# Block-sparse attention with a gated feed-forward layer on one core: value products in column halves, joint maxima, transposes without layout copies

## The chip, the cores and the metric

The kernel runs on one core of a Trainium2 chip. The core has a matrix engine (TensorE, called PE in the profile, with its weight loads as PEld), a vector engine (DVE), a scalar engine (ACT), a general engine (POOL) and a queue engine (SP). They run side by side, each taking its own instructions in the order in which the program lists them, and wait for each other by semaphores. TensorE writes to PSUM, eight banks of 512 fp32 columns on 128 partitions; DVE and ACT read it. The metric is the device time of one execution in microseconds.

## The reference

For 4 batches and 8 heads, 768 tokens and a head width of 64, scores are computed block by block (32 tokens). A row of blocks sees its own block, its neighbours, the first and the last block, and three sampled blocks. The first and the last row see everything. After the softmax and the product with V, the tokens go through a feed-forward layer with the activation h * sigmoid(beta * h).

```
scores = q @ k^T / sqrt(64)
mask = |bi - bj| <= 1  or  bi, bj in {0, 23}  or  bj in sampled[bi]
attn = softmax(where(mask, scores, -1e9));   x = attn @ v
x = x as [3072 tokens, 512]
h = x @ w_in            # [3072, 2048]
out = (h / (1 + exp(-beta * h))) @ w_out
```

## The kernel before

All work is described as tasks (class `Task`, lines 23 to 33) with an engine, an assumed duration, a priority, the tasks they depend on, and the PSUM banks that they open and close. `Plan.run` (lines 51 to 179) plays the tasks through once on the host and so fixes the order of every engine's instructions and the bank of every result: at each moment a free engine takes the task of the lowest priority number whose inputs and banks are there; a task whose banks are not free is passed over. The feed-forward tasks may hold at most 4 of the 8 banks while attention is left.

**Preparation of a batch.** K, Q and V arrive as fp16, 128 partitions by [head, 6 x 64], each partition holding six tokens. Batches 1 to 3 are loaded by POOL's queue in two halves each (line 443) into two buffers `RAW`, where Q takes V's. DVE copies (line 447) turn K and Q into `K16` and `Q16`, [6, 512] on each partition, so that two heads lie side by side. For batch 0 the loads go over SP and the cast from fp32 does the same (line 397). For each pair of heads, six full transposes on TensorE (lines 463 to 466) then fill a bank, and ACT or DVE copies it into `KT` or `QT` (line 470). V is rearranged by DVE (`vperm`), written to a table in device memory (`vtab`, line 494) and gathered from there for each pair of block rows over SP's queue (line 582).

**A pair of block rows**, n = 0 to 43, eleven in each batch:
- POOL and DVE gather eight K blocks for each row (`kg`, `kn`, lines 515 to 547).
- `sc` (line 595): 8 matmuls write the mask (L600) and 16 the scores (L610). Each uses 64 rows and 32 columns of the array at a tile position of its own; the heads of even and odd number (u = 0, 1) go to a bank each.
- `mx` (line 621): for each of the two banks one reduce on DVE, 128 partitions by 512, gives two negated maxima.
- `ex` (line 627): for each bank two exponentials on ACT with a sum each (L629).
- `rc`, `nrm`: reciprocal on DVE, four multiplications, mostly on POOL (L641).
- `tp`, `ptv`: eight transposes (L653), one copy out of PSUM (L657).
- `av` (line 661): 16 value products (L668). The stationary operand holds two heads' V, 128 columns; the moving one both heads' weights, 64 columns. Of the [128, 64] result only the blocks where the heads agree are used: rows 0 to 63 with columns of u = 0, rows 64 to 127 with those of u = 1.
- `xv` (line 678): the two useful quarters are therefore copied to `xT` one by one, 64 partitions by 256, each by DVE or ACT (L259 and L257, the lines of the helper `copy_on`).

**Global rows** (the first and the last block row, four units a batch, lines 691 to 777): scores over all 768 keys in two banks a unit (L705), two reduces of 384 and a third that joins them (L719, L721), two exponentials (L726), a sum and a reciprocal (L733, L734), a multiplication (L737), transposes (L745), and for the batch 24 products with V (`gav`, L758), copied to `xT` in four parts.

**Feed-forward**, in eight groups of 8 or 16 block rows: 16 slices of h (`h`, L817, 4 matmuls each), tanh on ACT (L823), the gate on DVE (L828), and per 128 tokens 64 matmuls into the output (`y`, L845), ACT's scaling (L263) and an output DMA on ACT's queue (L863). The activation is computed as h/2 * (1 + tanh(beta h / 2)).

Of the kernel before, what the change touches and what calls it, by code (L numbers as in the profile page):

```python
# [22 lines left out]
class Task:  # L23
    def __init__(self, name, eng, dur, emit, deps=(), prio=0.0, lat=0.0,
                 opens=(), closes=(), moe=False, dma=0.0, slack=0.0, hw=0, bulk=None):
        self.on = {eng: dur} if isinstance(eng, str) else dict(eng)
        self.name, self.eng, self.dur, self.emit = name, None, None, emit
        self.deps = [d for d in deps if d is not None]
        self.prio, self.lat = prio, lat
        self.opens, self.closes, self.moe, self.dma = opens, closes, moe, dma  # L30
        self.slack, self.hw, self.bulk = slack, hw, bulk
        self.kind = name.rstrip("0123456789.")
        self.end = None


class Plan:
# [9 lines left out]
    def add(self, *a, **k):  # L46
        t = Task(*a, **k)
        self.tasks.append(t)
        return t

    def run(self):
# [36 lines left out]
        while done < len(tasks):  # L88
            progress = False
            for e in engines:  # L90
# [3 lines left out]
                for t in waiting[e]:  # L94
# [9 lines left out]
                    if t.opens:  # L104
                        n_ok = sum(1 for f, _ in bank_free if f <= now + 1e-9)
                        if n_ok < len(t.opens):
                            continue
                        if t.moe and attention_left and held_moe + len(t.opens) > self.moe_banks:
                            continue
# [8 lines left out]
                if t.opens:  # L118
                    bank_free.sort()
                    for name in t.opens:  # L120
                        _, i = bank_free.pop(0)
# [61 lines left out]
def kernel(  # L183
# [14 lines left out]
    BLK = 32  # L198
# [32 lines left out]
    K16 = sb("K16", [P, J, D_MODEL])  # L231
    Q16 = sb("Q16", [P, J, D_MODEL])
    RAW = [sb(f"RAW{i}", [P, H, J * D]) for i in range(2)]
# [14 lines left out]
    banks = [psum.tile([P, 512], FP32, name=f"bank{i}") for i in range(8)]  # L248
# [4 lines left out]
    bank16 = lambda name: banks[plan.bank[name]][:, :].bitcast(FP16)  # L253

# [131 lines left out]
    for i, (nm, t, dst) in enumerate((("K", k, K16), ("Q", q, Q16), ("V", v, None))):  # L386
        for f in range(2):
# [6 lines left out]
            for hp in range(2 * f, 2 * f + 2):  # L394
# [3 lines left out]
                        out=dst[:, :, hp * P:(hp + 1) * P].rearrange("p j (h d) -> p h j d", h=2),  # L398
                        in_=stage32(i, hp).rearrange("p h (j d) -> p h j d", j=J)),
# [31 lines left out]
    trK, trQ, evK, evQ, vperm, vtab, perm = {}, {}, {}, {}, {}, {}, {}  # L431
    later = {b: [] for b in range(B)}
    for b in range(B):
        pr = prep_prio(b)
        if b:
            vperm[b] = []
            for nm, t, raw, dst in (("V", v, RAW[0], Vn[b % 2]), ("K", k, RAW[1], K16), ("Q", q, RAW[0], Q16)):
                tr = {"K": trK, "Q": trQ}.get(nm)
                for f in range(2):
                    hs = slice(f * HH, (f + 1) * HH)  # L440
                    free = [vperm[b][f]] if nm == "Q" else [perm["QK"["VK".index(nm)], b - 1, f]] if b > 1 else []
# [5 lines left out]
                    tpm = add(f"perm{nm}{b}.{f}", "DVE", 0.55, lambda raw=raw, dst=dst, hs=hs: copy_on(  # L447
                        "DVE", dst[:, :, hs.start * D:hs.stop * D].rearrange("p j (h d) -> p h j d", h=HH),
                        raw[:, hs, :].rearrange("p h (j d) -> p h j d", j=J)),
                        deps=[tl] + ([tr[b - 1, hp] for hp in range(2 * f, 2 * f + 2)] if tr else []),  # L450
                        prio=pr - 5 * (nm == "V"))
                    if nm == "V":
                        vperm[b].append(tpm)
                    else:
                        perm[nm, b, f] = tpm
                        for hp in range(2 * f, 2 * f + 2):
                            ld[nm, b, hp] = tpm
        for nm, s16, dstT, tr, ev in (("K", K16, KT, trK, evK), ("Q", Q16, QT, trQ, evQ)):
            for hp in range(NHP):
                def emit_tr(nm=nm, s16=s16, b=b, hp=hp):  # L460
                    o = bank16((nm, b, hp))
                    for j in range(J):
                        nc.tensor.transpose(  # L463
                            out=o[:, j * P:(j + 1) * P],
                            in_=s16[:, j, hp * P:(hp + 1) * P],
                            identity=identity)
# [36 lines left out]
    for n, (b, p) in enumerate(order_pairs):  # L503
# [91 lines left out]
        def emit_sc(n=n, b=b, p=p, i0=i0, kgb=kgb):  # L595
# [11 lines left out]
            for g in range(2):  # L607
                for hp in range(NHP):
# [9 lines left out]
                    opens=(("S", n, 0), ("S", n, 1)))  # L618

        for u in range(2):  # L620
            mx[n, u] = add(f"mx{n}.{u}", "DVE", 0.6, lambda n=n, u=u, sb_=sb_: nc.vector.tensor_reduce(  # L621
                out=sb_[:, 0, 2 * u:2 * u + 2],
                in_=bank(("S", n, u))[:, :].rearrange("x (g c) -> x g c", g=2),
                axis=AX.X, op=ALU.max, negate=True),
                deps=[sc[n]] + ([nrm[n - NP]] if n >= NP else []), prio=pr)

# [6 lines left out]
            ex[n, u] = add(f"ex{n}.{u}", "ACT", 0.91, emit_ex, deps=[mx[n, u]] + (  # L633
# [27 lines left out]
        def emit_av(n=n, vgb=vgb):  # L661
            o = bank(("O", n))
            pt = PT[n % NPT].rearrange("x (g c u m) -> x g c u m", g=2, c=2, u=2)
            first = True
            for g in range(2):
                for hp in range(NHP):
                    for c in range(2):
                        nc.tensor.matmul(  # L668
                            o[:, (g * NHP + hp) * 64:(g * NHP + hp + 1) * 64],
                            lhsT=vgb[:, g, c, hp * P:(hp + 1) * P],  # L670
                            rhs=pt[:, g, c, :, hp * BLK:(hp + 1) * BLK],
                            start=first, stop=(c == 1), skip_group_check=True)
                        first = False
        av[n] = add(f"av{n}", "PE", 0.47, emit_av, deps=[ptv[n], vres] + vg[n], prio=pr - 0.5, lat=0.2,
                    opens=(("O", n),))
        evs = []
        for u in range(2):
            def emit_xv(eng, n=n, u=u, b=b, i0=i0):
                src = bank(("O", n))[u * D:(u + 1) * D, :].rearrange(
                    "x (g h v m) -> x g h v m", g=2, h=NHP, v=2)[:, :, :, u, :]  # L680
                c0 = x_of(b * NB + i0)
                dst = xT[u * D:(u + 1) * D, :, c0:c0 + 2 * BLK].rearrange(
                    "x h (g m) -> x g h m", g=2)
                copy_on(eng, dst, src)
            evs.append(add(f"xv{n}.{u}", {"DVE": 0.42, "ACT": 0.38}, None, emit_xv, deps=[av[n]], prio=pr - 0.5,
                           closes=(("O", n),)))
# [7 lines left out]
    for b in range(B):  # L694
        for w, (blk, u) in enumerate((bl, u) for bl in (0, NB - 1) for u in range(2)):
# [15 lines left out]
            if u == 0:  # L711
                gs = add(f"gs{m}", "PE", 0.5, emit_gs, deps=[evK[b, hp] for hp in range(NHP)] +
                         [evQ[b, hp] for hp in range(NHP)], prio=pr, lat=0.2,
                         opens=tuple(("GS", m + uu, hf) for uu in range(2) for hf in range(2)))
                gsc_all.setdefault(b, []).append(gs)

            def emit_gm(m=m, s_=s_):
                for hf in range(2):
                    nc.vector.tensor_reduce(out=s_[:, hf:hf + 1], in_=bank(("GS", m, hf))[:, 0:S // 2],  # L719
                                            axis=AX.X, op=ALU.max, negate=True)  # L720
                nc.vector.tensor_reduce(out=s_[:, 2:3], in_=s_[:, 0:2], axis=AX.X, op=ALU.min)  # L721
            gm = add(f"gm{m}", "DVE", 1.15, emit_gm, deps=[gs] + ([gn[m - 2]] if m >= 2 else []), prio=pr)

            def emit_ge(m=m, s_=s_, pg=pg):
                for hf in range(2):
                    nc.scalar.activation(  # L726
                        out=pg[:, hf * (S // 2):(hf + 1) * (S // 2)], in_=bank(("GS", m, hf))[:, 0:S // 2],
                        func=AF.Exp, bias=s_[:, 2:3], scale=1.0, accum_out=s_[:, 3 + hf:4 + hf])
            ge = add(f"ge{m}", "ACT", 1.12, emit_ge, deps=[gm] + ([gt[m - 2]] if m >= 2 else []), prio=pr,
                     closes=(("GS", m, 0), ("GS", m, 1)))  # L730

            def emit_gr(s_=s_):
                nc.vector.tensor_reduce(out=s_[:, 5:6], in_=s_[:, 3:5], axis=AX.X, op=ALU.add)  # L733
                nc.vector.reciprocal(out=s_[:, 6:7], in_=s_[:, 5:6])  # L734
            gr = add(f"gr{m}", "DVE", 0.26, emit_gr, deps=[ge], prio=pr)
            gn[m] = add(f"gn{m}", {"POOL": 0.9, "DVE": 0.44}, None, lambda eng, s_=s_, pg=pg: (
                nc.vector if eng == "DVE" else nc.gpsimd).tensor_scalar(  # L737
                out=pg, in0=pg, scalar1=s_[:, 6:7], scalar2=1.0, op0=ALU.mult, op1=ALU.mult),
# [14 lines left out]
        def emit_gav(b=b):  # L753
            o = bank(("GO", b))
            first = True
            for hp in range(NHP):
                for j in range(J):
                    nc.tensor.matmul(  # L758
                        o[:, hp * P:(hp + 1) * P], lhsT=Vn[b % 2][:, j, hp * P:(hp + 1) * P],
                        rhs=PTG[:, j, :, hp * BLK:(hp + 1) * BLK],  # L760
                        start=first, stop=(j == J - 1), skip_group_check=True)
                    first = False
        gavt[b] = add(f"gav{b}", "PE", 1.4, emit_gav, deps=[gptv[gun - 4 + w] for w in range(4)] +
                      vperm[b], prio=pr, lat=0.2, opens=(("GO", b),))
        evs = []
        for u in range(2):
            def emit_gx(eng, u=u, b=b):
                src = bank(("GO", b))[u * D:(u + 1) * D, :].rearrange(
                    "x (h k v m) -> x h k v m", h=NHP, k=2, v=2)
                for kk, blk in enumerate((0, NB - 1)):  # L770
                    c0 = x_of(b * NB + blk)
                    dst = xT[u * D:(u + 1) * D, :, c0:c0 + BLK]
                    copy_on(eng, dst, src[:, :, kk, u, :])
            evs.append(add(f"gx{b}.{u}", {"DVE": 0.55, "ACT": 0.5}, None, emit_gx, deps=[gavt[b]], prio=pr,
                           closes=(("GO", b),)))
# [128 lines left out]
```

## Time and profile before

| | us |
|---|---|
| median of 3 runs | 320.73 (320.28 to 332.21) |
| the profiled execution | 323.59 |
| span of its instructions | 321.8 |
| PE busy | 280.7 |
| DVE busy | 246.7 |
| ACT busy | 216.8 |
| POOL busy | 187.5 |
| granted TensorE clock, mean | 0.929 |

The span reaches from the first to the last instruction of the profiled execution. Busy time is the time in which an engine had at least one instruction in flight; for TensorE, where matmuls are pipelined, it is more than the time in which the next could not have started. L and a number is a line of the kernel's file. A group's entry reads: line, engine, operation, output <- inputs, shapes, count, busy us and mean ns of one, idle time of the engine before these instructions, and what ended that. The chain of waits is followed back from the last instruction: at each step to what released it, or to the instruction before it on its engine.

### The profile page before, as it was taken

To read this page: it belongs to the slowest core of one execution; us is meant where nothing else is said; L and a number is where in the kernel's file an instruction comes from. 1 tells how busy PE (TensorE), PEld (TensorE's weight loads), DVE (VectorE), ACT (ScalarE), POOL (GpSimd) and SP (SyncE) were. 2 spreads that over 40 slices of the span, in tenths; PEclk is the share of its full clock that TensorE was granted. 3 is DMA by queue.
4 is the path that set the end of the run, shared out by engine and by line. 5 is a ranking of instruction groups with operands and counts; after the bars stand their busy time and mean duration, and the time that the engine had idled before them with its cause. 6 is when DMAs were issued, how large, how long until landed. Compare 5 with 4: busy or idle time off the path is not lost.

```text
span 321.8 us, 10665 instructions
## 1 busy us (share of the span) xinstructions
PE 280.7 (87%) x3525; PEld 177.3 (55%) x3525; DVE 246.7 (77%) x572; ACT 216.8 (67%) x644; POOL 187.5 (58%) x528
## 2 busy tenths in 40 slices
PE   0845578989979699988979999999999999999994
PEld 0612366956755486556635656555665555554671
DVE  2996579878869989999987667999979975771060
ACT  1676435864968489789687669977679864772361
POOL 2479956848778456798966654756948453200000
PEclk9975557999979989999979999999999999999999
DMA  7889995998697586323777973335232333100201
GB/s 255 332 172 208 229 227 105 187 252 177 132 204 145 164 212 114 107 80 94 125 146 168 226 170 93 88 84 153 94 118 69 91 110 100 33 3 33 98 2 66
DMA packets 42211, 43.97 MB, mean 137 GB/s; under 512 B 6440, under 2 KB 37672, under 8 KB 42156
## 3 DMA queue, kind: packets, MB, share of 16 engines
q1 hardware_dynamic: 27760, 25.71, 27.1%
q0 software_dynamic: 10784, 11.27, 23.4%
q10 hardware_dynamic: 3612, 6.30, 5.4%
q8 instruction: 28, 0.46, 0.6%
q14 instruction: 27, 0.22, 0.2%
HBM read 45.10 MB, written 9.44 MB: 169 GB/s over the span
## 4 chain that ended last, share of the span: by engine, by line
PE 60%; DMA 14%; DVE 12%; ACT 6%; issue 3%; SPq 3%; POOL 1%; POOLq 0%; ACTq 0%; DVEq 0%
PE bank L845 22%; PE bank L817 21%; DMA VG<-VT 6%; PE bank L668 4%; PE bank L653 4%; DMA RAW<-in_k_dram 3%; DMA VT<-Vn 3%; SPq L582 3%; DVE ST L621 2%; ACT PP L629 2%; PE bank L463 2%; DVE g L828 2%; PE bank L610 2%; PE bank L600 2%; DMA sbl<-in_sampled_blocks_dram 1%
## 5 line engine op out<-in xcount | busy, mean ns | idle before, releaser
L641 POOL TENSOR_SCALAR PP<-PP,ST 128x256 f16<-128x256 f16 x168 | 81.3, 501 | 47.9 <-DVE ST L635 42.4
L629 ACT ACTIVATE PP<-bank,ST 128x256 f16<-128x256 f32 x176 | 81.6, 478 | 30.1 <-DVE ST L621 21.5
L817 PE MATMUL bank<-xT,w_in_sb 128*128 128x256 f16 (+1 forms) x512 | 97.1, 338 | 3.9 <-ACT PP L629 1.1
L845 PE MATMUL bank<-w_out_sb,g 128*128 128x512 f16 x384 | 90.9, 380 | 0.0
L828 DVE SCALAR_TENSOR_TENSOR g<-t,bank 128x512 f16<-128x512 f16 (+1 forms) x128 | 66.6, 546 | 22.1 <-ACT t L823 21.3
L823 ACT ACTIVATE t<-bank,beta_sb 128x512 f16<-128x512 f32 (+1 forms) x128 | 69.9, 589 | 14.3 <-PE bank L817 11.6
L817 PEld LDWEIGHTS <-w_in_sb 128*128 128x128 f16 x512 | 55.3, 116 | 30.1 <-issue 8.6
L521 POOL COPY KG<-KT 128x64 f32 x264 | 54.6, 256 | 24.6 <-PE bank L610 17.8
L621 DVE TENSOR_REDUCE ST<-bank 128x2 f32<-128x512 f32 x88 | 57.5, 678 | 7.5 <-PE bank L610 7.4
L845 PEld LDWEIGHTS <-g 128*128 128x128 f16 x384 | 34.7, 98 | 38.6 <-issue 4.1
L668 PE MATMUL bank<-PT,VG 128*128 128x64 f16 x704 | 31.8, 199 | 7.9 <-DMA VG<-VT 5.9
L668 PEld LDWEIGHTS <-VG 128*128 128x128 f16 x704 | 28.3, 102 | 16.5 <-issue 9.6
L629 ACT ACTIVATION_READ_ACCUMULATOR PP<-bank,ST 128x1 f32 x176 | 36.8, 209 | 0.0
L653 PE MATMUL bank<-identity,PP 128*128 128x128 f16 x352 | 30.9, 233 | 6.6 <-ACT xT L257 2.4
L653 PEld LDWEIGHTS <-PP 128*128 128x128 f16 x352 | 24.6, 104 | 15.9 <-issue 4.1
L657 DVE COPY PT<-bank 128x1024 f16<-128x1024 f16 x44 | 30.1, 684 | 4.1 <-PE bank L653 3.3
L259 DVE CAST xT<-bank 64x256 f16<-64x256 f32 (+1 forms) x52 | 20.6, 402 | 12.3 <-PE bank L668 7.5
L263 ACT ACTIVATE osb<-bank 128x512 f32<-128x512 f32 x24 | 14.4, 601 | 20.7 <-PE bank L845 20.7
L257 ACT CAST xT<-bank 64x256 f16<-64x256 f32 (+1 forms) x52 | 17.4, 346 | 15.4 <-DVE xT L259 6.3
L610 PE MATMUL bank<-KG,QT 64*32 64x256 f16 x704 | 20.9, 293 | 1.4 <-POOL KG L521 1.0
L726 ACT ACTIVATE PG<-bank,SG 128x384 f16<-128x384 f32 x32 | 18.4, 583 | 4.9 <-DVE SG L721 4.1
L600 PE MATMUL bank<-maskr,ones 64*32 64x192 f16 (+1 forms) x352 | 14.9, 272 | 5.7 <-ACT PP L629 5.5
(79 smaller groups left out, 256.6 us busy)
## 6 DMA issues: line engine op xcount, KB each, us to landing
VG<-VT SPq DMA_DIRECT2D x268, 32.0 KB, 2.6
VG<-VT SPq DMA_DIRECT2D x40, 192.0 KB, 2.9
out_dram<-osb ACTq DMA_DIRECT2D x20, 256.0 KB, 2.2
RAW<-in_v_dram POOLq DMA_DIRECT2D x6, 384.0 KB, 5.1
RAW<-in_k_dram POOLq DMA_DIRECT2D x6, 384.0 KB, 5.6
VT<-Vn SPq DMA_DIRECT2D x3, 768.0 KB, 6.1
RAW<-in_q_dram POOLq DMA_DIRECT2D x6, 384.0 KB, 6.5
w_in_sb<-in_moe_w_in_dram POOLq DMA_DIRECT2D x8, 256.0 KB, 5.9
```

The lines of the kernel that those rows point to most:

```text
L521: nc.gpsimd.tensor_copy(out=kg32[:, g, :, (2 + r) * W:(3 + r) * W], in_=kt32[:, :, bass.ds(vals[3 * g + r], W)])
L610: nc.tensor.matmul(bk[u][hp * BLK:(hp + 1) * BLK, g * 256:(g + 1) * 256], lhsT=QT[b % 2][u * D:(u + 1) * D, hp, (i0 + g) * BLK:(i0 + g + 1 ...
L621: mx[n, u] = add(f"mx{n}.{u}", "DVE", 0.6, lambda n=n, u=u, sb_=sb_: nc.vector.tensor_reduce(out=sb_[:, 0, 2 * u:2 * u + 2], in_=bank(("S" ...
L629: nc.scalar.activation(out=pb[:, u, g, :], in_=bank(("S", n, u))[:, g * 256:(g + 1) * 256], func=AF.Exp, bias=sb_[:, 0, 2 * u + g:2 * u + ...
L641: (nc.vector if eng == "DVE" else nc.gpsimd).tensor_scalar(out=pb[:, u, g, :], in0=pb[:, u, g, :], scalar1=sb_[:, 2, 2 * u + g:2 * u + g + ...
L653: nc.tensor.transpose(out=o[:, s * P:(s + 1) * P], in_=pb[:, u, g, c * P:(c + 1) * P], identity=identity)
L657: ptv[n] = add(f"ptv{n}", "DVE", 0.61, lambda n=n: nc.vector.tensor_copy(out=PT[n % NPT], in_=bank16(("T", n))), deps=[tp[n]] + ([av[n - N ...
L668: nc.tensor.matmul(o[:, (g * NHP + hp) * 64:(g * NHP + hp + 1) * 64], lhsT=vgb[:, g, c, hp * P:(hp + 1) * P], rhs=pt[:, g, c, :, hp * BLK: ...
L817: nc.tensor.matmul(o[:, 0:TW], lhsT=w_in_v[:, c, f // 4, f % 4, :], rhs=xT[:, c, c0:c0 + TW], start=(c == 0), stop=(c == NHP - 1))
L823: lambda G=G, f=f, TW=TW, tt=tt: nc.scalar.activation(out=tt[:, 0:TW], in_=bank(("H", G, f))[:, 0:TW], func=AF.Tanh, bias=0.0, scale=beta_ ...
L828: lambda G=G, f=f, TW=TW, tt=tt, gg=gg: nc.vector.scalar_tensor_tensor(out=gg[:, f, 0:TW], in0=tt[:, 0:TW], scalar=1.0, in1=bank(("H", G, ...
L845: nc.tensor.matmul(o[:, :], lhsT=gg[:, f, s * P:(s + 1) * P], rhs=w_out_sb[:, f, :], start=(f == 0), stop=(f == N_FFC - 1))
```

## The change

Three things are done differently.

**Value products in two column halves.** `av` and `gav` issue two matmuls for each one of before, each for one head alone: 64 stationary columns, and 32 (64 for `gav`) moving ones, at tile positions (0, 0) and (0, 64). The useful results now fill 256 columns on all 128 partitions, and one copy takes them to `xT`. The last block row is computed ahead of the first, so that the global rows' two blocks are adjacent in `xT`.

**Joint maxima over two adjacent banks.** The banks become four tiles of two. `sc` and `gs` ask for pairs of adjacent banks (`twin=True`), which `choose` hands out; single banks are taken from broken pairs first. One reduce of 128 by 1024 gives a pair's four maxima, and both banks' exponentials wait for it. A global unit has one reduce, one exponential over 768 columns and one reciprocal.

**K and Q are transposed head by head as loaded.** The layout copies of K and Q are gone, and so are `K16` and `Q16`. Each head's [128, 64] piece is transposed by itself, 12 matmuls for a pair of heads, to 64 partitions each. K, Q and V have a buffer each; a half of K's or Q's is free for the next batch when its transposes are done.

The durations that the planner assumes stay at 0.36 us for a pair of heads' transposes, 0.47 for `av` and 1.4 for `gav`.

```diff
+    @staticmethod
+    def choose(t, bank_free, now):
+        at = {i: f for f, i in bank_free if f <= now + 1e-9}
+        whole = sorted((max(at[i], at[i + 1]), i) for i in at if i % 2 == 0 and i + 1 in at)
+        if t.twin:
+            if 2 * len(whole) < len(t.opens):
+                return None
+            return [i + h for _, i in whole[:len(t.opens) // 2] for h in range(2)]
+        if len(at) < len(t.opens):
+            return None
+        return sorted(at, key=lambda i: ((i ^ 1) in at, at[i], i))[:len(t.opens)]
...
-    K16 = sb("K16", [P, J, D_MODEL])
-    Q16 = sb("Q16", [P, J, D_MODEL])
-    RAW = [sb(f"RAW{i}", [P, H, J * D]) for i in range(2)]
+    RK, RQ, RV = (sb(f"R{x}", [P, H, J * D]) for x in "KQV")
...
-                    free = [vperm[b][f]] if nm == "Q" else [perm["QK"["VK".index(nm)], b - 1, f]] if b > 1 else []
+                    if tr is None:
+                        free = [vperm[b - 1][f]] if b > 1 else []
+                    else:
+                        free = [tr[b - 1, hp] for hp in hps]
...
                     for j in range(J):
-                        nc.tensor.transpose(
-                            out=o[:, j * P:(j + 1) * P],
-                            in_=s16[:, j, hp * P:(hp + 1) * P],
-                            identity=identity)
+                        for u in range(2):
+                            nc.tensor.transpose(
+                                out=o[u * D:(u + 1) * D, j * P:(j + 1) * P],
+                                in_=s16[:, 2 * hp + u, j * D:(j + 1) * D],
+                                identity=identity, tile_position=(0, u * D))
...
+        mx[n] = add(f"mx{n}", "DVE", 1.2, lambda n=n, sb_=sb_: nc.vector.tensor_reduce(
+            out=sb_[:, 0, :], in_=twin(("S", n, 0))[:, :, :].rearrange("x u (g c) -> x (u g) c", g=2),
+            axis=AX.X, op=ALU.max, negate=True),
+            deps=[sc[n]] + ([nrm[n - NP]] if n >= NP else []), prio=pr)
...
                     for c in range(2):
-                        nc.tensor.matmul(
-                            o[:, (g * NHP + hp) * 64:(g * NHP + hp + 1) * 64],
-                            lhsT=vgb[:, g, c, hp * P:(hp + 1) * P],
-                            rhs=pt[:, g, c, :, hp * BLK:(hp + 1) * BLK],
-                            start=first, stop=(c == 1), skip_group_check=True)
-                        first = False
+                        for u in range(2):
+                            us = slice(u * D, (u + 1) * D)
+                            nc.tensor.matmul(
+                                o[us, (g * NHP + hp) * BLK:(g * NHP + hp + 1) * BLK],
+                                lhsT=vgb[:, g, c, (2 * hp + u) * D:(2 * hp + u + 1) * D],
+                                rhs=pt[:, g, c, u, hp * BLK:(hp + 1) * BLK],
+                                start=(g + hp + c == 0), stop=(c == 1), skip_group_check=True,
+                                tile_position=(0, u * D))
...
-        for u in range(2):
-            def emit_xv(eng, n=n, u=u, b=b, i0=i0):
-                src = bank(("O", n))[u * D:(u + 1) * D, :].rearrange(
-                    "x (g h v m) -> x g h v m", g=2, h=NHP, v=2)[:, :, :, u, :]
...
+        def emit_xv(eng, n=n, b=b, i0=i0):
+            c0 = x_of(b * NB + i0)
+            copy_on(eng, xT[:, :, c0:c0 + 2 * BLK].rearrange("x h (g m) -> x g h m", g=2),
+                    bank(("O", n))[:, 0:2 * NHP * BLK].rearrange("x (g h m) -> x g h m", g=2, h=NHP))
...
+            gm = add(f"gm{m}", "DVE", 0.95, lambda m=m, s_=s_: nc.vector.tensor_reduce(
+                out=s_[:, 0:1], in_=twin(("GS", m, 0))[:, :, 0:S // 2], axis=AX.XY, op=ALU.max, negate=True),
+                deps=[gs] + ([gn[m - 2]] if m >= 2 else []), prio=pr)
+            ge = add(f"ge{m}", "ACT", 0.95, lambda m=m, s_=s_, pg=pg: nc.scalar.activation(
+                out=pg[:, :].rearrange("x (a c) -> x a c", a=2), in_=twin(("GS", m, 0))[:, :, 0:S // 2],
+                func=AF.Exp, bias=s_[:, 0:1], scale=1.0, accum_out=s_[:, 1:2]),
```

## The prediction

> **What bounds the kernel now.** I read the busy shares first, then three stretches, then the chain of waits inside each, then the groups by shape. The shares alone mislead:
>
> ```profile
> PE 280.7 (87%) x3525; PEld 177.3 (55%) x3525; DVE 246.7 (77%) x572; ACT 216.8 (67%) x644; POOL 187.5 (58%) x528
> ```
>
> TensorE looks like the bound everywhere. Busy time by stretch (start:end, then length, then busy us and instructions of each engine) tells three stages apart:
>
> ```profile
> 54.00:165.00 111.00, 99.40 (x1420) 70.18 (x1420) 99.00 (x234) 84.75 (x265) 82.46 (x221) 0.95 0.72 156
> 165.00:280.00 115.00, 114.62 (x1457) 65.86 (x1456) 93.20 (x196) 86.64 (x257) 69.28 (x203) 0.99 0.44 114
> 280.00:322.00 42.00, 37.21 (x218) 21.38 (x216) 14.75 (x30) 18.16 (x35) 0.00 (x0) 0.98 0.11 39
> ```
>
> I added the pieces of the chain of waits by engine. From 0 to 54 us it is DMA (29.3 us) and the SP queue (8.7). From 54 to 165 it is mixed: PE 38.8, DVE 27.8, ACT 17.0, DMA 15.9, unexplained issue 6.5. From 165 to the end it is PE for 150.5 of 157 us. So work taken from DVE or ACT pays only in the middle; TensorE time added after 165 us is paid in full.
>
> How long does TensorE take for a group? The chain gives it undisturbed (start, us, line, instructions):
>
> ```profile
> 200.56 0.47 PE bank L668 x16
> 201.03 0.21 PE bank L600 x8
> 201.23 0.22 PE bank L610 x16
> 201.45 2.71 PE bank L817 x12
> 204.16 0.45 PE bank L653 x8
> 204.61 0.86 PE bank L817 x4
> 205.47 0.21 PE bank L600 x8
> 205.68 0.22 PE bank L610 x16
> 205.90 0.57 PE bank L668 x16
> ```
>
> Two things are to be seen. L668, the value products, costs 0.47 us for 16, or 29 ns for each 64 streamed columns. And it costs 0.57 right behind L610. L600 and L610 use a tile position, 64 rows by 32 columns of the array; the others use all of it. Instruction by instruction, from 100 us on, a full-array matmul starts 2 to 3 ns after its forerunner's columns have passed (columns / 2.4 per ns, at granted clock 1.0). At each change between the two kinds it starts 94 to 97 ns after, entering and leaving alike (59 of 66 changes; the other seven waited longer, for something else). **A change of tile shape costs 0.095 us.**
>
> **What the change adds on TensorE.**
>
> Value products: 16 matmuls of 64 columns become 32 of 32 columns, in halves 64 wide, with a tile position. L610 shows that halves can run side by side: its matmuls of different positions start 3 ns apart, and each position is free again after 256/2.4 + 2.5 = 109 ns. So 16 steps per group. The step's price is not in the trace, since no 128x64 load is in it. From below it is 32/2.4 + 2.5 = 16 ns. From above: the four fp32 transposes of beta (L357) load 128 columns by a plain pattern and step 120 ns, so 60 ns for 64 columns. Nearest: a first matmul of L600 whose 32-column load was not fetched ahead takes 280 ns, one of L610 with the same 256 columns takes 269, so 32 columns cost 11 ns, 13 with the 2.5 of a start, and 64 about 27. I take 29 ns, the step of now: 16 x 29 = 0.47, unchanged, and two shape changes, 0.19.
>
> A rule of the Trainium skill speaks against this: "TensorEngine Tiling (Array Packing)", section Restrictions, says that column tiling switches off the fast weight load. "TensorE: Matmul & The Clock Gate", section LDWEIGHTS, prices a load at columns / 1.2 ns. By these pages the step would be an estimated 53 ns, and the group 0.85. The loads now have the chunked pattern and hide behind 27 ns of streaming; the new ones could not. That is rival two below, priced by L357's row.
>
> K and Q transposes: 6 per head pair become 12, in halves of 64 columns, 128 streamed each. A step of 128/2.4 + 2.5 = 56 ns covers any load up to that, so 0.33 stays, plus 0.19 per unbroken run of them.
>
> Products of the global rows: 24 of 128 columns (1.34 us) become 48 of 64, 24 steps of 29 = 0.70, with 0.19: 0.45 less for each of four.
>
> After 165 us there are 21 value groups (169.5 to 280.2 us). Three are followed by L600 and two preceded by L610, where one change exists already; about three touch K/Q transposes, of the same new shape. That leaves some 34 changes x 0.095 = 3.2. The last batch's transposes come in four runs: 0.5 after shared borders. One global product: -0.45. **Late sum: +3.3 us** (3.25). With 16 ns a step it is 3.3 - 21 x 16 x 0.013 = -1.1; with 60 ns 3.3 + 21 x 16 x 0.031 + 24 x 0.031 = +14.4.
>
> **What it removes on DVE and ACT.** The groups by shape (busy us, mean ns):
>
> ```profile
> L621 DVE TENSOR_REDUCE ST<-bank 128x2 f32<-128x512 f32 x88 | 57.5, 678 | 7.5 <-PE bank L610 7.4
> L259 DVE CAST xT<-bank 64x256 f16<-64x256 f32 x46 | 19.2, 418 | 11.8 <-PE bank L668 7.5 <-ACT xT L257 3.7
> L719 DVE TENSOR_REDUCE SG<-bank 128x1 f32<-128x384 f32 x32 | 16.1, 544 | 0.0
> L257 ACT CAST xT<-bank 64x256 f16<-64x256 f32 x42 | 15.4, 366 | 15.4 <-DVE xT L259 6.3 <-PE bank L668 6.0 <-DMA out_dram<-osb 2.8
> L259 DVE COPY K<-RAW 128x1536 f16<-128x1536 f16 x6 | 5.4, 897 | 1.8 <-DMA RAW<-in_k_dram 1.8
> ```
>
> In the middle stretch (18 pairs, eight global units, batches one and two prepared):
> - Joint maxima: the reduces of 512 and 384 elements (0.65 and 0.50 busy each) give 1.15 to 1.2 ns an element, or 1.04 by the means 678 and 544. 512 more cost 0.53. Two of 0.65 become 1.18: 18 x 0.12 = 2.1 DVE.
> - Copies of x: 50 there (DVE 8.4, ACT 8.9 us) become 21 of 0.4, as a 64-row copy of 256 elements takes what a 128-row one would: 4.4 less on each engine.
> - Layout copies of K and Q: four of 0.90 and four of 0.62, 6.1 DVE.
> - Global units: the two-bank reduce drops a 0.15 and one start, 0.25; the sum before the reciprocal goes, 0.12: 3.0 DVE for eight. ACT writes 768 in one, 2 x 0.57 becomes 0.57 + 384/1.2 ns = 0.89: 2.0 for eight.
>
> DVE loses 15.6 of 99 us, ACT 6.4 of 84.8. On the chain that is 16% of 27.8 = 4.4 and 7.5% of 17.0 = 1.3. After 165 us, where DVE loses much the same, it buys nothing: PE is late next.
>
> Two halves of one bank also wait for each other:
>
> ```profile
> ACT xT L257 <- DVE xT L259: 6.3, 11, 3.4
> DVE xT L259 <- ACT xT L257: 4.2, 8, 1.4
> ```
>
> (total us, times, longest.) At 107.4 to 110.1 us ACT stood 2.7 us; its x half went only after DVE had done the other at 109.7, behind a 1.9 us copy of K and two reduces. The chain puts that under an output DMA, but it goes with the halves: -2.7.
>
> **What it delays.** The first exponential now waits for 1.18 instead of 0.65. Behind it in ACT's queue stand tanh and x copies. The second half waits less in return, so it hurts where a single L621 stands in the chain ahead of an exponential: eight single pieces in the stretch, of which I count five: 5 x 0.53 = +2.6. Where an exponential was late anyway it costs 0.
>
> Score and global-score groups now need whole pairs of adjacent banks. The planner passes over a task whose banks aren't free, so it is planned later, and everything behind it. The nearest row is "PEld L600 <- issue", 11.6 us over 29 times, idle that nothing explains. Bounds: below 0 if every wish for a pair was granted, not under it, as the rule only narrows the choice; above another 11.6. As PE is 35% of the chain in the stretch and much of this idle lies elsewhere, I take +1.5.
>
> TensorE in the stretch: 18 groups x 0.19, ten runs of transposes x 0.19, three global products at -0.45: +4.0, of which its share of the chain, 35%, is +1.4.
>
> Loads: K and Q now have their own staging buffers, freed by transposes instead of copies. POOL issues the same 18 loads; Q no longer waits for V's rearranging. K of batch one still lands at 71.6 us and only the 0.56 copy behind it, counted above, goes. SP's queue keeps its order of table writes and gathers. Before 54 us DMA covers everything: 0; without that cover its five value groups would add 1.0.
>
> **Sum.** Middle: -4.4 - 1.3 - 2.7 + 2.6 + 1.5 + 1.4 = -2.9. Late: +3.3. Together +0.4 us on the profiled execution, 323.6 us (span 321.8). That execution is 0.9% above the median shown, 320.73; carried over, **321 us**.
>
> **Rivals.**
> 1. Faster. If DVE bounds the middle more than its chain share says (it is 89% busy, and the static order hands every late copy on), the whole 15.6 us leave, less half of the delays: about -13 + 3.3, 311 us. For it: the DVE block from 99 to 113 us, while no pair's score group ran from 96.0 to 118.0 us. Against: TensorE is 99.4 of 111 busy there. Chance 0.20.
> 2. Slower: half-width loads bound TensorE. 60 ns a step gives +14.4 late and, in the middle, 18 x 0.5 x 35% = +3 more: 335 us. It decides from a step above 35 ns, where the late loss passes 5.6 us and no gain of the middle covers it. For: L357's pattern; against: the 11 ns. Chance 0.20. If the two halves take turns as well (32 x 60 ns), 21 x 1.45 late, beyond 350 us: L610's 3 ns starts speak against it, 0.05.
> 3. Bank pairs starve the scores: +8 to +11.6 in the middle, 330 us; 0.13.
> 4. The change doesn't do what it says: layout copies vanish from the code for certain, but DVE's freed time may stay idle because the planned order (still 0.36, 0.47 and 1.4 us for the doubled TensorE groups) is wrong. Then the middle gains nothing: 324 us, inside the forecast.
>
> **Chances and range.** Forecast with rival 4, 315 to 327 us: 0.42. 2% is about what a measurement here can tell from no change. Faster by more: rival 1, 0.20. Slower: 0.20 + 0.05 + 0.13 = 0.38. The range must leave out at most 0.2: from 309 (rival 1 with a little to spare) to 338 (rival 2), which leaves the turns and the tails out.
>
> **What would show it.** Right: 0.66 us for 32 value products after 165 us, 95 ns at both borders; no K or Q copies; x copies near 0.4 us, one per pair; a 1.2 us reduce; PE still the chain after about 160 us. Wrong: 0.85 us or more per value group (rival 2); larger idle ahead of L600's successor (rival 3); a PE-only chain that begins clearly before 155 us (rival 1).

## The result, and the profile after

| | before | after |
|---|---|---|
| median, side by side on one chip (4 runs each) | 326.37 us (320.28 to 332.21) | 374.42 us (373.87 to 375.35) |
| ratio after / before | | 1.1685, 95% interval 1.164 to 1.173 |
| the profiled execution / its span | 323.59 / 321.8 us | 374.72 / 372.9 us |
| PE / DVE / ACT / POOL busy, us | 280.7 / 246.7 / 216.8 / 187.5 | 296.6 / 223.4 / 204.9 / 181.0 |

The change makes the kernel 17% slower; no change of time was forecast. Executions of one kernel spread by up to 4%; every ratio here compares its undisturbed executions alone, so it need not be the quotient of the medians beside it.

The page of the changed kernel: span, then busy time and share of each engine.

```profile
span 372.9 us, 12414 instructions
PE 296.6 (80%) x4517; PEld 182.5 (49%) x4517; DVE 223.4 (60%) x449; ACT 204.9 (55%) x585; POOL 181.0 (49%) x518
PE 46%; ACT 18%; DVE 11%; issue 5%; ACTq 1%; DVEq 0%
```

And the chain of the kernel before:

```profile
PE 60%; DMA 14%; DVE 12%; ACT 6%; issue 3%; SPq 3%; POOL 1%; POOLq 0%; ACTq 0%; DVEq 0%
```

DVE and ACT have less to do, by 23 and 12 us, as planned. Yet each engine is busy for a smaller share of the time than before: TensorE had nothing in flight for 372.9 - 296.6 = 76.3 us, against 321.8 - 280.7 = 41.1. The third line is the chain of waits by engine; in the changed kernel it could be followed back to 68 us only, which is why its shares don't add up to 100%. PE's fell from 60% to 46%. Of the 51.1 us that the span grew, 35.2 are such idle time. The other 15.9 are time in flight, of which only 3.8 stay in the version with single tiles (284.5 us) that follows below, though it has the same matmuls. This kernel waits more than it computes more.

Where? Busy time of each engine by stretch (start:end, length, then PE, PEld, DVE, ACT, POOL, granted clock, DMA share, GB/s) in the changed kernel:

```profile
54.00:165.00 111.00, 95.16 (x1790) 65.16 (x1787) 80.73 (x170) 70.52 (x220) 70.35 (x201) 0.98 0.70 149
165.00:330.00 165.00, 142.01 (x2112) 79.92 (x2111) 100.76 (x174) 98.21 (x273) 78.29 (x220) 1.00 0.33 87
330.00:373.00 43.00, 33.08 (x176) 18.06 (x175) 10.04 (x23) 14.08 (x28) 0.00 (x0) 1.00 0.10 37
```

TensorE had been busy 114.62 of 115 us between 165 and 280; now it stands idle for 23 of 165 there, and for 10 of 43 in the end, where nothing is left but the feed-forward part (4.8 of 42 before). The granted clock is 1.00: not the reason. On the chain, PE held 150.5 of the last 157 us before. After 165 us it now holds 120.4 of 208, and ACT 47.1, DVE 22.5, unexplained issue 12.6 hold the rest.

Which waits are new? Lines from the list of waits of the changed kernel, and below them two lines of the kernel before (who waits, for whom: total us, times, longest):

```profile
DVE g L822 <- ACT t L817: 36.3, 32, 16.8
ACT t L817 <- DVE g L822: 19.1, 26, 1.9
PE bank L811 <- ACT t L817: 9.5, 17, 1.3
DVE g L822 <- PE bank L811: 6.5, 10, 1.3
PE bank L811 <- DVE g L822: 4.8, 7, 1.6
PE bank L839 <- ACT osb L275: 3.9, 7, 0.7
```

```profile
DVE g L828 <- ACT t L823: 21.3, 19, 14.0
ACT t L823 <- DVE g L828: 0.2, 1, 0.2
```

A gate reads the tanh, so the first line is natural (21.3 us before). The second is new: a tanh reads a bank of h and writes a buffer `t`, and before it waited for a gate once in the whole kernel, for 0.2 us. The fourth has no reason in the data: the gate reads `t`, which is made from h, so when the tanh is done h is long there; before there was no such wait. TensorE's idle time ahead of h and y tells the same (groups by line, from the page):

```profile
L811 PE MATMUL bank<-xT,w_in_sb 128*128 128x256 f16 (+1 forms) x512 | 99.5, 334 | 18.8 <-ACT t L817 9.5
L839 PE MATMUL bank<-w_out_sb,g 128*128 128x512 f16 x384 | 93.3, 379 | 14.5 <-ACT osb L275 3.9
```

The same two before (L817 and L845 there):

```profile
L817 PE MATMUL bank<-xT,w_in_sb 128*128 128x256 f16 (+1 forms) x512 | 97.1, 338 | 3.9 <-ACT PP L629 1.1
L845 PE MATMUL bank<-w_out_sb,g 128*128 128x512 f16 x384 | 90.9, 380 | 0.0
```

The two lines hold 29.4 of the 35.2 us that TensorE lost to idleness, in instructions that the change doesn't touch.

The timeline of the last feed-forward group shows it at work (start, length, engine, line, what, count, idle before):

```profile
353.12 1.21 ACT L817 ACTIVATE t<-bank,beta_sb 128x256 f16<-128x256 f32 x3 [0.42 <-ACT osb L275]
353.64 1.47 PE L811 MATMUL bank<-xT,w_in_sb 128*128 128x256 f16 x12 [0.71 <-ACT t L817]
354.35 1.08 DVE L822 SCALAR_TENSOR_TENSOR g<-t,bank 128x256 f16<-128x256 f16 x3 [16.83 <-ACT t L817]
354.80 1.23 ACT L817 ACTIVATE t<-bank,beta_sb 128x256 f16<-128x256 f32 x3 [0.48 <-DVE g L822]
355.33 1.47 PE L811 MATMUL bank<-xT,w_in_sb 128*128 128x256 f16 x12 [0.21 <-ACT t L817]
356.03 1.08 DVE L822 SCALAR_TENSOR_TENSOR g<-t,bank 128x256 f16<-128x256 f16 x3 [0.60 <-ACT t L817]
```

And in the kernel before:

```profile
303.15 4.09 PE L817 MATMUL bank<-xT,w_in_sb 128*128 128x256 f16 x36
304.42 3.03 ACT L823 ACTIVATE t<-bank,beta_sb 128x256 f16<-128x256 f32 x8 [0.47 <-PE bank L817]
304.93 2.25 DVE L828 SCALAR_TENSOR_TENSOR g<-t,bank 128x256 f16<-128x256 f16 x6 [13.98 <-ACT t L823]
```

In the changed kernel three engines go in lockstep: three tanhs, then three gates, then three tanhs, with 12 matmuls at a time between. The first gate starts at 354.35; its own tanh had ended at 353.59. What ended just before it were four of TensorE's matmuls, of another slice of h (354.24), and the third tanh (354.32); the trace lists semaphores of both engines as what this gate waited for. The 64 matmuls of h of this group take 9.24 us from the first start to the last; before they took 6.88.

### The profile page after: what moved, and what is told of

Its sections match the earlier page's. It is cut to its first block, busy times and chain, and to the rows that moved or that the text cites. A ratio compares the mean times of both kernels' runs of the same rounds, so it can differ in the third digit from the quotient of the medians.

```text
span 372.9 us, 12414 instructions
## 1 busy us (share of the span) xinstructions
PE 296.6 (80%) x4517; PEld 182.5 (49%) x4517; DVE 223.4 (60%) x449; ACT 204.9 (55%) x585; POOL 181.0 (49%) x518
## 4 chain that ended last, share of the span: by engine, by line
PE 46%; ACT 18%; DVE 11%; issue 5%; ACTq 1%; DVEq 0%
PE bank L839 22%; PE bank L811 11%; ACT t L817 7%; ACT PP L639 6%; DVE g L822 5%; PE bank L679 5%; ACT osb L275 3%; PE bank L663 2%; PE bank L475 2%; DVE PT L667 2%; DVE ST L632 1%; PE bank L742 1%; DVE KT L271 1%; PE bank L622 1%; PE bank L612 1%
## 5 line engine op out<-in xcount | busy, mean ns | idle before, releaser
L651 POOL TENSOR_SCALAR PP<-PP,ST 128x256 f16<-128x256 f16 x168 | 79.1, 487 | 92.1 <-DVE ST L645 92.0
L811 PE MATMUL bank<-xT,w_in_sb 128*128 128x256 f16 (+1 forms) x512 | 99.5, 334 | 18.8 <-ACT t L817 9.5
L839 PE MATMUL bank<-w_out_sb,g 128*128 128x512 f16 x384 | 93.3, 379 | 14.5 <-ACT osb L275 3.9
L817 ACT ACTIVATE t<-bank,beta_sb 128x512 f16<-128x512 f32 (+1 forms) x128 | 69.6, 583 | 45.0 <-DVE g L822 19.1
L533 POOL COPY KG<-KT 128x64 f32 x264 | 52.2, 247 | 24.9 <-PE bank L622 16.0
L632 DVE TENSOR_REDUCE ST<-bank 128x4 f32<-128x1024 f32 x44 | 53.2, 1213 | 5.5 <-PE bank L622 5.5
L667 DVE COPY PT<-bank 128x1024 f16<-128x1024 f16 x44 | 30.3, 688 | 38.4 <-PE bank L663 15.6
L679 PE MATMUL bank<-PT,VG 128*64 128x32 f16 x1408 | 34.0, 187 | 11.5 <-DMA VG<-VT 5.7
L679 PEld LDWEIGHTS <-VG 128*64 128x64 f16 x1408 | 30.5, 116 | 24.6 <-issue 17.0
L269 ACT CAST xT<-bank 128x256 f16<-128x256 f32 x30 | 11.2, 372 | 27.5 <-PE bank L679 15.4
L726 ACT ACTIVATE PG<-bank,SG 128x768 f16<-128x768 f32 x16 | 14.5, 912 | 10.9 <-DVE SG L723 5.3
L734 POOL TENSOR_SCALAR PG<-PG,SG 128x768 f16<-128x768 f16 x13 | 12.1, 932 | 15.2 <-DVE SG L731 15.2
```

Of the source, the lines that this page charges most:

```text
L533: nc.gpsimd.tensor_copy(out=kg32[:, g, :, (2 + r) * W:(3 + r) * W], in_=kt32[:, :, bass.ds(vals[3 * g + r], W)])
L632: mx[n] = add(f"mx{n}", "DVE", 1.2, lambda n=n, sb_=sb_: nc.vector.tensor_reduce(out=sb_[:, 0, :], in_=twin(("S", n, 0))[:, :, :].rearrang ...
L651: (nc.vector if eng == "DVE" else nc.gpsimd).tensor_scalar(out=pb[:, u, g, :], in0=pb[:, u, g, :], scalar1=sb_[:, 2, 2 * u + g:2 * u + g + ...
L667: ptv[n] = add(f"ptv{n}", "DVE", 0.61, lambda n=n: nc.vector.tensor_copy(out=PT[n % NPT], in_=bank16(("T", n))), deps=[tp[n]] + ([av[n - N ...
L679: nc.tensor.matmul(o[us, (g * NHP + hp) * BLK:(g * NHP + hp + 1) * BLK], lhsT=vgb[:, g, c, (2 * hp + u) * D:(2 * hp + u + 1) * D], rhs=pt[ ...
L811: nc.tensor.matmul(o[:, 0:TW], lhsT=w_in_v[:, c, f // 4, f % 4, :], rhs=xT[:, c, c0:c0 + TW], start=(c == 0), stop=(c == NHP - 1))
```

## The experiments

Three theories stood. **T1**: the banks are now declared as four tiles of two, and the program keeps accesses to one tile in order, even where they touch different banks of it. So two results that merely share a tile wait for each other. **T2**: the planner's order, or its choice of banks, is worse. **T3**: TensorE's half-width products are slower than they look. The two kernels of the first pair are mirror images.

### The declaration alone, on the kernel before

Same instructions, same order, same bank numbers as before; only the eight banks become halves of four tiles.

```diff
-    banks = [psum.tile([P, 512], FP32, name=f"bank{i}") for i in range(8)]
+    twins = [psum.tile([P, 2, 512], FP32, name=f"bank{i}") for i in range(4)]
+    banks = [twins[i // 2][:, i % 2, :] for i in range(8)]
```

> The kernel before, with one edit: its eight banks are declared as four tiles of two banks, as in the change; every engine's instructions and the bank of every result stay as they were. Theory T1 (the two banks of one tile are kept apart like one object, so an access to one bank waits for accesses to the other): 1.08 to 1.17 of before, and PE waits on ACT and DVE in the last 40 us, where before it ran without a gap. Rival T2 (the order and the choice of adjacent banks, made by the planner, cost the time): 0.99 to 1.01. Rival T3 (half-width matmuls and shape changes cost it): 0.99 to 1.01.

Measured: 386.15 against 327.26 us, ratio 1.173 (1.157 to 1.188). The whole loss is there, with nothing computed differently; it lies a hair above the 1.17 that T1 gave as its upper end. The same odd waits are there:

```profile
ACT t L824 <- DVE g L829: 11.7, 16, 1.3
DVE g L829 <- PE bank L818: 11.4, 14, 1.4
```

### The change, with eight tiles of one bank

The change's order and its bank numbers stay. A joint instruction is written on one tile, so each is issued as two: the pair's reduce, the global unit's reduce (with the third that joins them), its exponential, and the sum ahead of the reciprocal.

```diff
-    twins = [psum.tile([P, 2, 512], FP32, name=f"bank{i}") for i in range(4)]
-    banks = [twins[i // 2][:, i % 2, :] for i in range(8)]
+    banks = [psum.tile([P, 512], FP32, name=f"bank{i}") for i in range(8)]
...
+            for u in range(2):
+                nc.vector.tensor_reduce(
+                    out=sb_[:, 0, 2 * u:2 * u + 2],
+                    in_=bank(("S", n, u))[:, :].rearrange("x (g c) -> x g c", g=2),
+                    axis=AX.X, op=ALU.max, negate=True)
```

> The changed kernel with its order and its bank numbers, but eight tiles of one bank each; the joint reduces and the joint exponential are therefore issued as two again (for a global unit three small ones more), in the same places. T1: 0.97 to 1.03 of before. T2: 1.10 to 1.17, as the order is that of the change. T3: 1.10 to 1.17, as all half-width matmuls are there.

Measured: 327.65 against 327.26 us, ratio 0.9985 (0.989 to 1.008). The loss is gone, though order, bank numbers and half-width products are those of the change. T2 and T3 fall as causes of it. Its stretches (columns as above) and its last feed-forward group:

```profile
54.00:165.00 111.00, 104.39 (x1975) 70.84 (x1973) 96.36 (x234) 84.65 (x265) 78.22 (x214) 1.00 0.73 158
165.00:280.00 115.00, 115.00 (x1844) 64.88 (x1843) 82.89 (x176) 82.35 (x246) 67.42 (x199) 1.00 0.43 113
280.00:322.00 42.00, 35.88 (x214) 20.53 (x208) 13.71 (x28) 16.55 (x32) 0.00 (x0) 0.98 0.11 39
```

```profile
301.82 4.86 PE L822 MATMUL bank<-xT,w_in_sb 128*128 128x256 f16 x43
303.09 3.77 ACT L828 ACTIVATE t<-bank,beta_sb 128x256 f16<-128x256 f32 x10 [0.47 <-PE bank L822]
303.60 2.98 DVE L833 SCALAR_TENSOR_TENSOR g<-t,bank 128x256 f16<-128x256 f16 x8 [13.98 <-ACT t L828]
```

From 165 to 280 us TensorE is busy 115 of 115 us again, and the 64 matmuls take 6.88 us: 43 of them, ten tanhs and eight gates run without a break in any of the three engines. The first gate follows its own tanh.

### One pair of banks as one tile

If T1 holds, the loss should grow with the number of banks so declared. On the kernel before, banks 0 and 1 alone:

```diff
-    banks = [psum.tile([P, 512], FP32, name=f"bank{i}") for i in range(8)]
+    twins = [psum.tile([P, 2, 512], FP32, name=f"bank{i}") for i in range(1)]
+    banks = [twins[0][:, i, :] for i in range(2)] + [
+        psum.tile([P, 512], FP32, name=f"bank{i}")[:, :] for i in range(2, 8)]
```

> The kernel before with banks 0 and 1 alone declared as one tile of two; six tiles of one bank; the same instructions, order and banks. T1 as a sum over pairs: a quarter of the loss of four such tiles, 1.03 to 1.06. If one late engine holds up all others through the static order, more than a quarter: 1.06 to 1.12. Without an effect of the tile: 0.99 to 1.01.

Measured: 339.06 against 327.9 us, ratio 1.040 (1.033 to 1.047): a quarter of the 0.173 of four, which would be 0.043. The group of 64 takes 7.69 us. Its list of waits has the odd pairs in small:

```profile
DVE g L830 <- ACT t L825: 24.8, 20, 14.0
ACT t L825 <- DVE g L830: 3.6, 6, 1.0
DVE g L830 <- PE bank L819: 2.5, 3, 1.3
PE bank L819 <- DVE g L830: 2.0, 4, 0.8
```

The trace also lists the semaphores that each instruction waits for, and these count the same way. Of the 128 gates, those that wait for a semaphore of TensorE are 1 before and 2 in the change with single tiles; 13 with one pair tile, 39 with four on the kernel before, 40 in the change.

### Value products and x copies alone

The kernel before with the value products in halves, one copy of x, and the last block row first.

```diff
+                        for u in range(2):
+                            nc.tensor.matmul(
+                                o[us, (g * NHP + hp) * BLK:(g * NHP + hp + 1) * BLK],
+                                lhsT=vgb[:, g, c, (2 * hp + u) * D:(2 * hp + u + 1) * D],
...
+                                tile_position=(0, u * D))
...
+            copy_on(eng, xT[:, :, c0:c0 + 2 * BLK].rearrange("x h (g m) -> x g h m", g=2),
+                    bank(("O", n))[:, 0:2 * NHP * BLK].rearrange("x (g h m) -> x g h m", g=2, h=NHP))
```

> The kernel before with the value products (pairs and global rows) in column halves and x copied at once, nothing else. The prediction's steps: 0.66 us for 32 value products, +3.3 us late, x copies halved for -2.7 and some of DVE and ACT in the middle: 0.99 to 1.02. T3: above 1.05. T1 and T2 say nothing against 0.99 to 1.02.

Measured: 333.91 against 327.26 us, ratio 1.020 (1.007 to 1.032). A little slower alone. Its chain (start, length, what) has one piece as long as the loss:

```profile
162.13 0.85 POOL PG L733
162.98 6.54 DMA RAW<-in_v_dram
169.54 0.56 DVE Vn L259
```

The load of batch 3's V, issued on POOL's queue behind that multiplication, is waited for 6.54 us. One profile shows it, and no run took it away: argued, not shown.

### Transposes alone

The kernel before with K and Q loaded into buffers of their own, no layout copies, 12 transposes a head pair.

```diff
-    K16 = sb("K16", [P, J, D_MODEL])
-    Q16 = sb("Q16", [P, J, D_MODEL])
-    RAW = [sb(f"RAW{i}", [P, H, J * D]) for i in range(2)]
+    RK, RQ, RV = (sb(f"R{x}", [P, H, J * D]) for x in "KQV")
```

> The kernel before with K and Q transposed head by head as loaded, without layout copies, with three staging buffers, nothing else. The prediction's steps: 0.33 us for 12 transposes and 0.19 for each run of them, DVE 9 us less in all: 0.98 to 1.01. T3: above 1.03, with transposes that take 0.6 us or more for a pair of heads.

Measured: 322.32 against 327.26 us, ratio 0.989 (0.979 to 0.999). That looked like a gain, so it ran again, in five rounds:

> The transposes as loaded alone, once more in more rounds, since it was the only part that came out below before (0.989, upper end 0.999). If that was real: 0.98 to 0.995 with an upper end below 1; if it was the spread between runs: 0.995 to 1.005.

Measured: 323.19 against 325.26 us, ratio 1.000 (0.995 to 1.006). No gain: the first answer was chance.

### Both of these together

> The kernel before with the column halves and the transposes as loaded, no joint maxima, no pairs of banks, the planner's own choice of banks as before. If the parts' effects simply add (1.02 and 0.99): 1.00 to 1.02. If the order and the choice of banks made for pairs were a cost hidden in the run with the change's order and single tiles (T2 in small): clearly below that run's 0.9985, 0.97 to 0.985.

Measured: 327.99 us (322.38 to 331.21, four executions), where the kernel before had 327.9 beside it. The medians show no difference. There is no ratio with an interval for this run, so it doesn't decide between the two expectations.

### Joint instructions with only as many pair tiles as the scores need

All three parts. Banks 0 to 3 are two pair tiles, handed out in pairs for scores; everything else prefers four single tiles.

```diff
-    twins = [psum.tile([P, 2, 512], FP32, name=f"bank{i}") for i in range(4)]
-    banks = [twins[i // 2][:, i % 2, :] for i in range(8)]
+    twins = [psum.tile([P, 2, 512], FP32, name=f"bank{i}") for i in range(2)]
+    banks = [twins[i // 2][:, i % 2, :] for i in range(4)] + [
+        psum.tile([P, 512], FP32, name=f"bank{i}")[:, :] for i in range(4, 8)]
```

> The changed kernel with all three parts, joint reduces and joint exponential included, but only banks 0 to 3 are declared as two tiles of two, and scores alone ask for them; the other tasks prefer the four tiles of one bank and break a pair only when none is free. T1 (a tile's two banks wait for each other): most of the loss goes, 0.98 to 1.04, as the two banks of a score group are written and read together anyway and only few other results share such a tile. If the joint reduce itself, or the wait of the first exponential for it, cost the time: 1.08 or more.

Measured: 334.5 against 327.9 us, ratio 1.019 (1.005 to 1.032). Most of the loss is gone, but there is no gain: PE holds 158.5 us of the chain after 165 us, and only 1 gate waits for a semaphore of TensorE. The 64 matmuls take 6.90 us.

The same with value products as before, since those alone had cost 2%:

> The same, but the value products and the copies of x as before: joint maxima over two pairs of banks and transposes as loaded. T1: 0.97 to 1.03; below the run with the halves, if these are a cost as they are by themselves (1.02), above it if the x copies saved are worth more than the shape changes.

Measured: 332.48 us, ratio 1.012 (1.000 to 1.025). No better that can be told. Joint maxima found no arrangement here in which they pay. Why is not separated: with two pairs in place of four, the scores also have fewer banks to choose from.

### Truer durations for the planner

The planner assumed 0.36 us for transposes that take 0.55, and 0.47 for value products that take 0.71. The transposes alone, told 0.55:

> The same with the planner told the measured 0.55 us for the transposes of a pair of heads in place of 0.36. If the planner's wrong duration costs time through the static order: 0.5% or more below the run beside it; if not: within 0.5% of it.

Measured: 329.23 against 325.26 us, ratio 1.011 (0.997 to 1.024). That is neither of the two expected, and the interval holds 1: undecided. And the single-tile version with 0.71, 0.55, and 0.95 for the global products:

```diff
-        av[n] = add(f"av{n}", "PE", 0.47, emit_av, deps=[ptv[n], vres] + vg[n], prio=pr - 0.5, lat=0.2,
+        av[n] = add(f"av{n}", "PE", 0.71, emit_av, deps=[ptv[n], vres] + vg[n], prio=pr - 0.5, lat=0.2,
```

> The change with eight tiles of one bank (joint instructions issued as two), and the planner told the measured times: 0.71 us for 32 value products, 0.55 for transposes, 0.95 for the global products, in place of 0.47, 0.36 and 1.4. If the rest of the change was held back by the planned order: below 0.985. If TensorE's extra time for shape changes takes what DVE and ACT gain, as the prediction's sum has it: 0.985 to 1.01.

Measured: 335.45 against 325.26 us, ratio 1.044 (1.035 to 1.053). Clearly slower, against what was expected. Its chain from 54 to 165 us is PE 37.9, ACT 19.2, DVE 16.9, DMA 15.6 us, where with the old durations ACT was 3.5 and DVE 10.0; after 165 us DMA still has 7.6. The order came out worse; why truer durations make a worse one stays open.

## Why the prediction was wrong, by its own steps

**The failed step** is this sentence: "Score and global-score groups now need whole pairs of adjacent banks." It priced the pairs as a question of which banks are free, between below 0 and +11.6 us, and took +1.5; rival 3 went to 330 us by the same thought. The place was right, mechanism and size were not: the version with single tiles asks for the same pairs of banks, in the same order, and loses nothing. The cost is in the declaration, `twins = [psum.tile([P, 2, 512], ...`, a line of the diff that no step priced. With it alone the ratio is 1.173, without it 0.9985. On 320.73 us, 17% is some 54 us, more than three times the distance from the forecast to the upper end of the range.

**How it works.** In the code as written nothing forbids a gate in bank 2 while TensorE fills bank 3. The program is given semaphore waits for accesses that share a tile, and from then on it does. h takes a bank for each slice; tanh, gate and the next matmuls meet in neighbouring halves, and each waits for the other two. In the middle of the kernel score groups and h slices can be neighbours too, which fits with ACT's new share of the chain: tanhs have 7% and exponentials 6% (2% before). That part is argued.

The Trainium skill ("PSUM — Partial Sum Buffer", section PSUM bank collisions raise a hardware error) asks for a guard by bank and by group of 32 partitions; it reports that two engines at work in different banks run clean. So the chip, by that page, asks for no wait between a gate in one bank and matmuls in the other. The runs agree as far as they go: with one tile a bank, the three engines overlapped (timeline above).

**There was a clue.** The prediction showed "ACT xT L257 <- DVE xT L259: 6.3" and used it as a gain: two engines that read different partitions of one bank wait for each other. That fits the same rule, order kept by tile and not by the bytes touched. No run separates it from two others, order kept by bank, or by the output tile `xT` that both copies write. But the question what else must wait, asked of every tile that the diff declares, would have led to the loss.

**Without that step the total came out, in part by luck.** The version with single tiles has no joint instructions, else the change: 0.9985 x 320.73 = 320.2 us (317 to 323), where 321 had been forecast. That is no proof of the sum: this version lacks the joint instructions, with their gains and delays, and its middle did not go as forecast (below). The prices of single steps were near (the first five rows are of the single-tile version, the others of the change):

| term | forecast | measured |
|---|---|---|
| value group, 32 products | 0.66 us | 0.71 (median of 32 groups) |
| a step of two halves, side by side | 29 ns | 32 ns |
| a shape change | 95 ns | 95 in, 102 out |
| transposes of a head pair | 0.52 us | 0.55 |
| global products | 0.89 us | 0.89 to 0.97 |
| joint reduce | 1.18 us | 1.21 |
| x copy | 0.4 us | 0.37 ACT, 0.42 DVE |
| exponential of a global unit | 0.89 us | 0.91 |

The value group is to be read in the chain of the single-tile version (start, length, line, instructions): 0.61 us, and 0.10 on the piece behind.

```profile
200.70 1.73 PE bank L822 x8
202.42 0.61 PE bank L681 x32
203.03 0.21 PE bank L610 x8
...
206.31 1.73 PE bank L822 x8
208.04 0.61 PE bank L681 x32
208.65 1.83 PE bank L850 x8
```

And the rows of reduce, exponential and copies in the changed kernel (groups; busy us, mean ns):

```profile
L632 DVE TENSOR_REDUCE ST<-bank 128x4 f32<-128x1024 f32 x44 | 53.2, 1213 | 5.5 <-PE bank L622 5.5
L726 ACT ACTIVATE PG<-bank,SG 128x768 f16<-128x768 f32 x16 | 14.5, 912 | 10.9 <-DVE SG L723 5.3 <-PE bank L742 1.8 <-POOL PP L651 1.5
L269 ACT CAST xT<-bank 128x256 f16<-128x256 f32 x30 | 11.2, 372 | 27.5 <-PE bank L679 15.4
L271 DVE CAST xT<-bank 128x256 f16<-128x256 f32 x18 | 7.5, 418 | 10.9 <-PE bank L679 6.2 <-ACT osb L275 3.3 <-PE bank L839 0.7
```

**Middle stretch.** Forecast: DVE's and ACT's pieces on the chain shrink, 4.4 and 1.3 us and 2.7 for the x halves. With single tiles they shrank more, DVE from 27.8 to 10.0 and ACT from 17.0 to 3.5 us. But DMA grew from 15.9 to 27.9, POOL from 3.3 to 10.7 and the SP queue from 0.1 to 7.4: what is late next took much of it. The prediction asked that question only for the time after 165 us.

**Rival 1** (faster, 311 us): DVE did lose its work, and no run is faster by 2%. **Rival 2** (half-width loads, 335 us): a step of 32 ns, below the 35 from which it was to decide (where the late loss, by the prediction's own terms, is 5.4 us and not 5.6); in the single-tile version the chain after 165 us is PE for 150.9 of 155 us, as it was. The 53 ns estimated from the Trainium skill ("TensorE: Matmul & The Clock Gate", section LDWEIGHTS) are not borne out by that step. **Turns**: refuted, the starts of the 32 products come 3 to 4 and 28 to 29 ns apart by turns, which makes 16 steps. **Rival 3** (pairs starve the scores, 330 us): it named the right part by the wrong mechanism, see above. **Rival 4** (nothing gained in the middle, 324 us): not decided. With single tiles TensorE stood idle for 6.6 of the 111 us between 54 and 165, where it had been 11.6, but the granted clock of that stretch was 1.00 in this execution and 0.95 in that of the kernel before, so how much of it the change gained stays open.

## What to carry to other kernels

In these runs a tile of two PSUM banks is the unit by which the program keeps order, not the bank. Before declaring two banks, buffers or halves as one tile for the sake of one joint instruction, therefore, list everybody else who will use a part of it, and ask which pairs of engines now wait for each other; one pair among the eight banks cost 4% here. And when the trace shows a wait that the data doesn't explain, find its rule first and then apply it to what the change adds, not only to what it removes.

## What the runs showed that was not expected

The price of the pair tiles: 1.040 for one of four, 1.173 for all. Which kind of neighbours costs most, two readers or a reader and a writer, was not separated, and a joint reduce across two single tiles was not tried.

Two 64-column halves of TensorE take 32 ns a step, with 32 columns streamed in each, and the change back to the full array 102 ns where 95 had been seen. And the planner: the transposes with a truer duration 1.011 (0.997 to 1.024), all three 1.044 (1.035 to 1.053). The first is undecided. In the second, an order found with wrong durations was better than the one with right ones (0.9985, in another series of runs), and a new order alone moved the time by 4%, some 14 us, where the prediction's whole sum had come to 0.4.
